# Loads of queries, keys and values moved from SyncE's queue to GpSimd's in an attention and mixing kernel

## The chip, the cores and the metric

The kernel runs on one core of a Trainium2 chip. A core has five engines that work side by side, each through its own instructions in order: TensorE (PE: matrix products, with a weight load ahead of each), VectorE (DVE), ScalarE (ACT), GpSimd (POOL) and SyncE (SP), which here only begins transfers. Transfers run on 16 DMA engines; an instruction on some engine begins one, and a semaphore tells when it has landed. The metric is the device time of one execution in microseconds (us).

## The reference

The program has three stages: attention with pooled queries, a low-rank mixing with a multilayer perceptron, and a gated block with spatial mixing. All is float32 from outside.

```python
# q, k, v: (4, 8, 1152, 64); S = 1152, factor = 2
q_pool = q.reshape(B, H, S // 2, 2, D).mean(axis=3)
scores = (1 / sqrt(D)) * q_pool @ k^T
attn = softmax(scores)                      # sum + 1e-9 in the denominator
x = attn @ v                                # -> (4, 576, 512)
# second stage
h = x^T @ U @ V                             # rank 32 over the sequence
u = x + h^T
x = u + relu(u @ w_ch1) @ w_ch2             # 512 -> 2048 -> 512
# third stage
h = relu(x @ w_in); u, v = halves of h
v_n = (v - mean) / sqrt(var + 1e-6)
out = (u * (w_spatial @ v_n + b_spatial)) @ w_out
```

## The kernel before

The 32 heads are handled as 16 pairs. A pair is nine units of work, one for each 128 rows of pooled queries of one head (the ninth holds the last 64 rows of both heads). The pairs 0 to 4 (`SP = 5`) go another way (`peak`, `turn`, `weigh`); the change concerns the pairs 5 to 15.

For such a pair, `pair_load` begins the transfers of the keys (`kP`, 128 x 1152 float32) and of the queries (`qP`, the two halves to be pooled, 128 x 2 x 576), and `v_load` that of the values (128 x 1152); each is 576 KB. There is one buffer of each kind for these pairs: `r_kraw.items[0]`, the single one of `r_qraw`, and `r_vraw.items[0]`. A load therefore has to wait until the pair before has read its buffer for the last time. `pair_prep` reads keys and queries: ScalarE rounds the keys and VectorE takes the rest (`dve.tensor_sub(kl, raw, kh)`), GpSimd adds the two halves of the queries in place (`pool.tensor_add`), ScalarE and VectorE make a high and a low part of the sum, and GpSimd copies their last columns to `padl`. `v_prep` reads the values: VectorE finds the largest, ScalarE makes the high float16 part and VectorE the low one.

In `scores` TensorE makes the scores of a unit, VectorE finds each row's maximum, ScalarE takes the exponent and rounds it to a high float16 half; the low half is the rest. In units with `lifted(i)` GpSimd makes the low half, in the others VectorE:

```python
act.copy(p16[:, 0, :], p32)
pool.tensor_sub(p16[:, 1, :], p32, p16[:, 0, :])
...
sp.dma_start_transpose(out=pt, in_=p16.rearrange("p a b -> p (a b)"))
```

A transposing transfer, begun by SyncE, turns both halves into `pt`, and `pv` multiplies it by the values on TensorE. Two buffers `p16` and three buffers `pt` go round. Between the units run the perceptron of earlier heads (`mlp1`), its weight loads and its stores to `x2d`, which SyncE begins too.

The order is planned. Nothing is issued at once: `rec` (a `Recorder`) records every operation with its engine, its estimated cost and what it depends on. At the end of the attention stage `issue` plans all recorded operations 83 times (`ORDERS`), each time handing every engine the operation of least key among those that are ready, keeps the best plan, and then walks the list `done` in the planned order and calls the real engine. The instructions of an engine follow each other in that order, and each waits for its semaphores in its turn. In the plan a plain load occupies SyncE for 390 ns and a transposing one for 2790 ns.

All recorded operations are issued from one line, L379, so the profile's groups are told apart by tile: `at` holds the attention's buffers (`kraw`, `qraw`, `vraw`, `p32`, `p16`, `pt` and others), `ml` the perceptron's, `co` small things and weights, `ps` is PSUM, `in_kP_dram`, `in_qP_dram` and `in_v_dram` are the inputs.

Of the kernel before, what the change touches and what calls it, by code (L numbers as in the profile page):

```python
# [24 lines left out]
NP = H // 2  # L25
# [9 lines left out]
SP = 5  # L35
# [56 lines left out]


class Op:
    __slots__ = ("eng", "calls", "cost", "prio", "deps", "users", "left", "ready", "start", "end", "n", "dma", "late", "port", "fly", "lanes", "wide")


class Recorder:
# [51 lines left out]
    def begin(self, eng):  # L150
        op = Op()
        op.eng, op.calls, op.cost, op.prio = eng, [], 0.0, self.prio
        op.deps, op.users, op.n, op.dma, op.start = set(), [], len(self.ops), 0.0, None
        op.port, op.fly, op.lanes, op.wide = False, 0.0, None, False
        self.ops.append(op)
        return op

# [196 lines left out]
    def issue(self, passes=0, later=None):  # L354
        ops, self.ops = self.ops, []
        self.mine = set(ops)
        for op in ops:
            for d in op.deps:
                if d in self.mine:
                    d.users.append(op)  # L360
        key = lambda o: (o.prio, o.n)
        best = None
        for i in range(passes or ITER):
            done, state = self.forward(ops, key)
            end = max(o.end for o in ops)
            if best is None or end < best[0] or i == passes - 1:
                best = (end, done, state, [(o.start, o.end) for o in done])
            self.backward(ops)
            key = (lambda o: (o.late, o.n)) if i % 2 else (lambda o: (o.prio >= 0, o.late, o.n))
        end, done, (self.free, self.dma, self.load, self.port, self.sides), times = best  # L370
        for op, t in zip(done, times):
            op.start, op.end = t
        self.predicted = end
        if later:
            done = self.fill(done, later)
        for op in done:
            eng = getattr(self.nc, op.eng)
            for method, args, kwargs in op.calls:
                getattr(eng, method)(*args, **kwargs)  # L379

# [38 lines left out]
def tile_kernel(ctx: ExitStack, tc: tile.TileContext, qD, kD, qP, kP, v, U, V, w1, w2, w_in, spT, bsp, w_out, out):  # L419
    nc = tc.nc  # L420
    ctx.enter_context(tc.manual_schedule())
    rec = Recorder(nc)
    dve, act, pool, pe, sp = rec.vector, rec.scalar, rec.gpsimd, rec.tensor, rec.sync
# [78 lines left out]
    def flat(t):  # L502
        return t.rearrange("p a b c -> p (a b c)")[:, :2 * KC * D]
# [16 lines left out]
    wide = psum.rearrange("p a b -> p (a b)")  # L520
# [161 lines left out]
    def pair_load(pr):  # L682

        kraw[2 * pr] = t = r_kraw.items[0]
        sp.dma_start(out=t, in_=kP[pr - SP])
        qraw[2 * pr] = t = r_qraw.next()
        sp.dma_start(out=t, in_=qP[pr - SP])

    def pair_prep(pr):

# [33 lines left out]
    def v_load(pr):  # L724
        if pr < SP:
            vraw[pr] = t = r_vraw.items[1] if pr == NP else r_vraw.next()
            src = v[pr // NP, pr % NP].rearrange("p e (c d) -> p e c d", c=KC)
            for e in range(2):
                sp.dma_start(out=t[:, e, :, 0:D], in_=src[:, e])
        else:  # L730
            vraw[pr] = t = flat(r_vraw.items[0]).rearrange("p (e n) -> p e n", e=2)
            sp.dma_start(out=t, in_=v[pr // NP, pr % NP])

    def v_prep(pr):
        if pr < SP:
# [356 lines left out]
    k_load(1)  # L1092
    q_load(1)
    v_load(0)
    rec.prio = 1
    q_prep(1)
# [18 lines left out]
    for pr in range(1, SP):  # L1115
        s0 = 9 * pr
        on(s0 - 9, s0 - 9, k_load, 2 * pr)
        on(s0 - 8, s0 - 8, q_load, 2 * pr)
        on(s0 + 1 if pr == NP else s0 - 7, s0 - 7, v_load, pr)

        on(s0 - 3, s0 - 4, q_prep, 2 * pr)
        on(s0 - 3, s0 - 4, k_prep, 2 * pr)
        on(s0 - 5, s0 - 5, k_load, 2 * pr + 1)
        on(s0 - 3, s0 - 5, q_load, 2 * pr + 1)
        on(s0 + 1, s0, q_prep, 2 * pr + 1)
        on(s0 + 1, s0, k_prep, 2 * pr + 1)
    for pr in range(SP, B * NP):
        s0 = 9 * pr
        t = pr == SP
        on(s0 - 7 if t else s0 - PL, s0 - PL, pair_load, pr)  # L1130
        on(s0 - 7, s0 - 7, v_load, pr)
        on(s0 - 3 if t else s0 - PP, s0 - PP + PQ, pair_prep, pr)
        on(s0 + 1 if t else s0 - VP, s0 - VP + VQ, v_prep, pr)
# [451 lines left out]
```

## Time and profile before

| | us |
|---|---|
| median of 3 runs | 1019.08 |
| lowest and highest of them | 1018.6, 1021.37 |
| the profiled execution | 1017.92 |
| its span in the profile | 1016.2 |
| TensorE busy | 974.9 (96%) |
| VectorE busy | 800.3 (79%) |
| ScalarE busy | 663.9 (65%) |
| GpSimd busy | 256.8 (25%) |

Busy times are sums over the instructions of an engine. Instructions that begin a transfer, semaphore and branch instructions are not counted as busy; they appear with their own times in a timeline (SPq is SyncE's queue). Matmuls are pipelined and their ends are modelled, so a busy TensorE is not one at its peak. Nearly all transfers of this kernel run on one queue, q1, which SyncE feeds: 137.47 MB in 270656 packets, 58.4% of the time of 16 DMA engines.

### The profile page before, as it was taken

To read this page: it belongs to the slowest core of one execution; us is meant where nothing else is said; L and a number is where in the kernel's file an instruction comes from. 1 tells how busy PE (TensorE), PEld (TensorE's weight loads), DVE (VectorE), ACT (ScalarE), POOL (GpSimd) and SP (SyncE) were. 2 spreads that over 40 slices of the span, in tenths; PEclk is the share of its full clock that TensorE was granted. 3 is DMA by queue.
4 is the path that set the end of the run, shared out by engine and by line. 5 is a ranking of instruction groups with operands and counts; after the bars stand their busy time and mean duration, and the time that the engine had idled before them with its cause. 6 is when DMAs were issued, how large, how long until landed. Compare 5 with 4: busy or idle time off the path is not lost.

```text
span 1016.2 us, 26412 instructions
## 1 busy us (share of the span) xinstructions
PE 974.9 (96%) x10983; PEld 803.5 (79%) x10983; DVE 800.3 (79%) x1664; ACT 663.9 (65%) x1238; POOL 256.8 (25%) x213
## 2 busy tenths in 40 slices
PE   7898999999999999999999999999999999999998
PEld 6687788878777877788877787888778788888887
DVE  6978888889998797898677968867598849885670
ACT  7777977787775666766666666656386637575522
POOL 1333532243323413142233323221000003200300
PEclk8999999999999999999999999999999999999999
DMA  9654154299769958788896968677643031531002
GB/s 330 199 182 131 53 172 135 87 217 228 131 123 186 189 111 190 153 156 166 158 192 113 188 118 150 119 146 126 195 137 93 25 135 43 151 99 43 11 2 94
DMA packets 270776, 139.16 MB, mean 137 GB/s; under 512 B 248160, under 2 KB 253152, under 8 KB 269632
## 3 DMA queue, kind: packets, MB, share of 16 engines
q1 hardware_dynamic: 270656, 137.47, 58.4%
q8 instruction: 86, 1.41, 0.6%
q14 instruction: 34, 0.28, 0.1%
HBM read 69.09 MB, written 9.44 MB: 77 GB/s over the span
## 4 chain that ended last, share of the span: by engine, by line
PE 59%; DVE 13%; ACT 8%; DMA 6%; issue 3%; SPq 0%; POOL 0%; ACTq 0%; DVEq 0%
PE ps L379 59%; DVE co L379 6%; ACT at L379 6%; DMA at<-at 5%; DVE at L379 3%; DVE ml L379 3%; ACT ma L379 1%; ACT ml L379 1%; DVE ma L379 1%; DMA ma<-in_bsp_dram 1%; SPq L379 0%; POOL at L379 0%; DMA at<-in_w_dram 0%; ACT co L379 0%; ACT L379 0%
## 5 line engine op out<-in xcount | busy, mean ns | idle before, releaser
L379 PE MATMUL ps<-at,at 128*64 128x65 f32 (+6 forms) x2892 | 240.0, 277 | 9.9 <-ACT at L379 8.3
L379 DVE TENSOR_REDUCE co<-ps 128x1 f32<-128x1152 f32 (+1 forms) x169 | 201.2, 1195 | 52.3 <-PE ps L379 31.5
L379 POOL TENSOR_TENSOR at<-at 128x1152 f16<-128x1152 f32 (+1 forms) x74 | 162.7, 2202 | 285.2 <-ACT at L379 179.4
L379 PEld LDWEIGHTS ps<-at,at 128*64 128x64 f32 (+2 forms) x2892 | 190.6, 160 | 42.6 <-ACT at L379 19.5
L379 PEld LDWEIGHTS <-co 128*128 128x128 f16 x1872 | 177.6, 98 | 53.8 <-issue 15.1
L379 PE MATMUL ps<-ml,co 128*128 128x288 f16 x1344 | 180.3, 286 | 6.2 <-DVE ml L379 4.5
L379 PE MATMUL ps<-ml,ml 128*128 128x288 f16 x1344 | 180.0, 287 | 1.8 <-DVE co L379 1.2
L379 PEld LDWEIGHTS <-ml 128*128 128x128 f16 x1536 | 145.7, 98 | 41.7 <-issue 6.6
L379 ACT ACTIVATE at<-ps,co 128x1152 f32<-128x1152 f32 x99 | 120.7, 1219 | 86.7 <-DVE co L379 80.4
L379 ACT CAST at<-at 128x1152 f16<-128x1152 f32 (+3 forms) x96 | 99.6, 1050 | 20.8 <-DMA at<-at 13.8
L379 PE MATMUL ps<-ma,ma 128*128 128x288 f16 (+2 forms) x676 | 105.0, 318 | 0.0
L379 PEld LDWEIGHTS <-at 128*128 128x128 f16 (+1 forms) x2970 | 89.3, 101 | 10.2 <-issue 5.1
L379 PE MATMUL ps<-at 128*128 128x64 f16 (+1 forms) x2970 | 93.4, 194 | 1.6 <-DVE at L379 0.8
L379 ACT ACTIVATE at<-ps 128x640 f32<-128x640 f32 (+4 forms) x132 | 70.0, 555 | 26.5 <-PE ps L379 25.7
L379 PE MATMUL ps<-at,co 128*128 128x288 f16 (+4 forms) x481 | 72.8, 299 | 0.2 <-DVE at L379 0.2
L379 ACT ACTIVATE at<-at 128x1152 f16<-128x1152 f32 (+1 forms) x55 | 58.6, 1065 | 9.4 <-DMA at<-at 7.7
L379 DVE SCALAR_TENSOR_TENSOR at<-at 128x1152 f16<-128x1152 f32 x44 | 59.4, 1351 | 3.8 <-ACT at L379 2.1
L379 ACT ACTIVATE ml<-ps 128x288 f16<-128x288 f32 (+1 forms) x96 | 38.9, 408 | 31.2 <-PE ps L379 30.8
L379 DVE SCALAR_TENSOR_TENSOR ml<-ml,co,ml 128x288 f16<-128x288 f32 (+1 forms) x80 | 52.9, 686 | 3.0 <-ACT ml L379 3.0
L379 PEld LDWEIGHTS <-ma 128*128 128x128 f16 x448 | 43.7, 98 | 11.4 <-issue 0.5
L379 ACT ACTIVATE ml<-ml,co 128x288 f16<-128x288 f32 (+2 forms) x91 | 47.5, 571 | 6.0 <-DVE co L379 5.7
L379 ACT CAST ma<-ma 128x288 fp32r<-128x288 f32 (+4 forms) x62 | 27.4, 465 | 34.1 <-DVE ma L379 34.1
(108 smaller groups left out, 1278.2 us busy)
## 6 DMA issues: line engine op xcount, KB each, us to landing
ml<-in_w_dram SPq DMA_DIRECT2D x8, 1024.0 KB, 6.3
at<-in_v_dram SPq DMA_DIRECT2D x11, 576.0 KB, 4.7
at<-in_qP_dram SPq DMA_DIRECT2D x11, 576.0 KB, 4.7
at<-in_kP_dram SPq DMA_DIRECT2D x11, 576.0 KB, 5.0
at<-in_qD_dram SPq DMA_DIRECT2D x10, 576.0 KB, 4.4
at<-in_kD_dram SPq DMA_DIRECT2D x10, 576.0 KB, 6.0
ml<-in_w_dram SPq DMA_DIRECT2D x8, 512.0 KB, 5.8
at<-in_w_dram SPq DMA_DIRECT2D x8, 512.0 KB, 4.7
```

Source lines behind the costliest of these rows:

```text
L379: getattr(eng, method)(*args, **kwargs)
```

## The change

`Op` gets one more field, `to`. Where it is set, `issue` calls that engine and not the one that the operation was planned for. `pair_load` sets it to GpSimd for keys and queries, and `v_load` for the values of the pairs from 5 on: 33 loads in all. The plan is made as before, with these loads on SyncE, and the order of the list `done` stays; only the queue is another one. In GpSimd's stream such a load stands between those of GpSimd's operations that the list has before and after it. The source of a load is put into a variable first, which changes nothing that is executed.

```diff
--- before.py
+++ after.py
@@ -92,7 +92,7 @@
 
 
 class Op:
-    __slots__ = ("eng", "calls", "cost", "prio", "deps", "users", "left", "ready", "start", "end", "n", "dma", "late", "port", "fly", "lanes", "wide")
+    __slots__ = ("eng", "calls", "cost", "prio", "deps", "users", "left", "ready", "start", "end", "n", "dma", "late", "port", "fly", "lanes", "wide", "to")
 
 
 class Recorder:
@@ -151,7 +151,7 @@
         op = Op()
         op.eng, op.calls, op.cost, op.prio = eng, [], 0.0, self.prio
         op.deps, op.users, op.n, op.dma, op.start = set(), [], len(self.ops), 0.0, None
-        op.port, op.fly, op.lanes, op.wide = False, 0.0, None, False
+        op.port, op.fly, op.lanes, op.wide, op.to = False, 0.0, None, False, None
         self.ops.append(op)
         return op
 
@@ -374,7 +374,7 @@
         if later:
             done = self.fill(done, later)
         for op in done:
-            eng = getattr(self.nc, op.eng)
+            eng = getattr(self.nc, op.to or op.eng)
             for method, args, kwargs in op.calls:
                 getattr(eng, method)(*args, **kwargs)
 
@@ -682,9 +682,13 @@
     def pair_load(pr):
 
         kraw[2 * pr] = t = r_kraw.items[0]
-        sp.dma_start(out=t, in_=kP[pr - SP])
+        s = kP[pr - SP]
+        sp.dma_start(out=t, in_=s)
+        rec.ops[-1].to = "gpsimd"
         qraw[2 * pr] = t = r_qraw.next()
-        sp.dma_start(out=t, in_=qP[pr - SP])
+        s = qP[pr - SP]
+        sp.dma_start(out=t, in_=s)
+        rec.ops[-1].to = "gpsimd"
 
     def pair_prep(pr):
 
@@ -729,7 +733,9 @@
                 sp.dma_start(out=t[:, e, :, 0:D], in_=src[:, e])
         else:
             vraw[pr] = t = flat(r_vraw.items[0]).rearrange("p (e n) -> p e n", e=2)
-            sp.dma_start(out=t, in_=v[pr // NP, pr % NP])
+            s = v[pr // NP, pr % NP]
+            sp.dma_start(out=t, in_=s)
+            rec.ops[-1].to = "gpsimd"
 
     def v_prep(pr):
         if pr < SP:
```

## Rows read from the trace of the kernel before

**Rows 1.** Window 150 to 720: PE, PEld, DVE, ACT, POOL; clock; DMA

```profile
150.00:720.00 570.00, 553.07 (x7051) 451.17 (x7051) 469.08 (x883) 384.65 (x661) 178.91 (x139) 1.00 0.77 155
```

**Rows 2.** Waits, 150 to 720 us: us in total, times, longest

```profile
POOL at L379 <- DMA at<-in_qP_dram: 26.2, 7, 6.3
ACT at L379 <- DMA at<-at: 21.5, 23, 3.4
PE ps L379 <- DVE co L379: 5.5, 6, 1.4
PE ps L379 <- DVE ml L379: 4.8, 7, 1.4
DVE co L379 <- DMA at<-in_v_dram: 4.0, 3, 2.6
PE ps L379 <- DMA at<-at: 0.7, 2, 0.5
```

**Rows 3.** DMA issues: times, KB each, median us from issue to landing

```profile
at<-in_v_dram SPq DMA_DIRECT2D x11, 576.0 KB, 4.7
at<-at SPq DMA_TRANSPOSE x99, 4.8
```

**Rows 4.** SyncE's instructions on queries: ns min/median/max, first and last start

```profile
L379 SPq DMA_DIRECT2D at<-in_qP_dram x11: 328/382/1476, 162.1 to 565.5; - x11
```

**Rows 5.** SyncE's timeline: start, us, what, times

```profile
473.48 0.53 SPq L379 DMA_DIRECT2D at<-in_v_dram  x1
474.10 0.38 SPq L379 DMA_DIRECT2D at<-in_qP_dram  x1
474.59 5.34 SPq L379 DMA_TRANSPOSE at<-at  x1
479.98 0.57 SPq L379 DMA_DIRECT2D at<-in_kP_dram  x1
480.65 13.26 SPq L379 DMA_TRANSPOSE at<-at  x3
...
519.53 0.53 SPq L379 DMA_DIRECT2D at<-in_v_dram  x1
520.17 4.11 SPq L379 DMA_TRANSPOSE at<-at  x1
...
618.36 51.62 SPq L379 DMA_TRANSPOSE at<-at  x11
```

**Rows 6.** VectorE's timeline: the last readers of load buffers

```profile
249.60 1.35 DVE L379 TENSOR_TENSOR at<-at,at 128x1152 fp32r<-128x1152 f32 x1
...
437.54 1.34 DVE L379 TENSOR_TENSOR at<-at,at 128x1152 fp32r<-128x1152 f32 x1
...
469.11 1.39 DVE L379 SCALAR_TENSOR_TENSOR at<-at,co,at 128x576 f16<-128x576 f32 x1
...
564.72 0.74 DVE L379 SCALAR_TENSOR_TENSOR at<-at,at 128x576 fp32r<-128x576 f32 x1
```

**Rows 7.** GpSimd's timeline, and ScalarE's first reader of queries

```profile
251.21 2.38 POOL L379 TENSOR_TENSOR at<-at 128x1152 f16<-128x1152 f32 x1 [2.97 <-ACT at L379]
...
434.66 1.41 POOL L379 TENSOR_TENSOR at<-at 128x576 f32<-128x576 f32 x1
438.11 3.01 POOL L379 TENSOR_TENSOR at<-at 128x1152 f16<-128x1152 f32 x1 [2.04 <-ACT co L379]
...
565.22 2.48 POOL L379 TENSOR_TENSOR at<-at 128x1152 f16<-128x1152 f32 x1 [7.72 <-ACT at L379]
...
468.30 0.68 ACT L379 ACTIVATE at<-at 128x576 fp32r<-128x576 f32 x1
```

**Rows 8.** Groups by form, 150 to 720: us, mean ns, idle before

```profile
L379 POOL TENSOR_TENSOR at<-at 128x1152 f16<-128x1152 f32 x55 | 133.5, 2430 | 239.4 <-ACT at L379 179.4 <-ACT co L379 37.7 <-DVE co L379 18.1
L379 DVE SCALAR_TENSOR_TENSOR at<-at 128x1152 f16<-128x1152 f32 x44 | 59.4, 1351 | 3.8 <-ACT at L379 2.1 <-ACT co L379 0.9 <-issue 0.4
L379 DVE TENSOR_SCALAR ml<-ml 128x512 int32<-128x512 int32 x12 | 5.8, 487 | 1.2 <-ACT ml L379 1.2
```

## The prediction

> **What bounds the kernel now.** I read the page first, then the window of the stretch that the change touches, then who waits for whom there, and last the single instructions around the loads. The 33 loads that move (queries, keys and values of pairs 5 to 15) and all transposing transfers lie between 150 and 720 us. In these 570 us TensorE is busy 553.07, so 16.9 us of its time are free [rows 1]. That is nearly the whole prize: whatever an edit speeds up here, it can hardly give back more. The list of waits says what TensorE waits for: mostly results of VectorE (5.5 and 4.8 us in the two largest groups) and, for 0.7 us, a transposing transfer [rows 2]. No load stands in it.
>
> The loads are waited for by others: GpSimd stood 26.2 us for queries, VectorE 4.0 us for values [rows 2]. GpSimd's wait looks large, but it has work for 178.91 of the 570 us only [rows 1], and what it waits for isn't urgent: the queries that it adds up at 434.66 are first read by ScalarE at 468.30 [rows 7], 32 us after the addition ended. So the path runs through scores, maximum, exponent, cast, subtraction, transpose and product, and the loads lie beside it.
>
> **Part 1: what SyncE loses.** One issue of a load takes SyncE 0.38 us in the median [rows 4]; 33 of them are 12.5 us of its time. SyncE's queue is worked in order, so a transpose behind a load pays for it only if its data were ready. In most places they weren't. I found three with no other reason: the transpose at 474.59 follows two loads that hold SyncE from 473.48 to 474.48, the one at 480.65 a load that ends at 480.55, the one at 520.17 a load that ends at 520.06 [rows 5]. Without the loads these three start 1.1, 0.7 and 0.6 us sooner, 2.4 us together. What that is worth: ScalarE waited for a transpose 23 times [rows 2], against 99 transposes [rows 3], so about 23 / 99 = 0.23 of such a shift reaches anyone: 0.6 us. Bounds: 0 and 2.4.
>
> **Part 2: loads that begin sooner.** A load waits for the last reader of its buffer. One buffer of values was free at 469.11 + 1.39 = 470.50 [rows 6], and SyncE, busy with transposes, began the load at 473.48 [rows 5]: 3 us late. From GpSimd's queue it can begin when the buffer is free, if GpSimd is. Of VectorE's 4.0 us of waiting for values all may go. VectorE is idle 570 - 469.08 = 100.9 us in the window [rows 1], and TensorE waited 5.5 + 4.8 = 10.3 us for it [rows 2]: 10.3 / 100.9 = 0.10 of an idle microsecond of VectorE is felt. So 0.4 us are gained. Bounds: 0 and 4.0. Queries have 32 us to spare and gain nothing.
>
> **Part 3: what GpSimd gains in work.** No row shows a load begun by GpSimd. Below, the nearest row is SyncE's issue of the same load, 0.38 us [rows 4]; above, GpSimd's own commonest instruction, a subtraction over 128 x 1152, at 2.43 us [rows 8]. I take 1.0 us, near their geometric mean: a begin moves no data through the engine, as the first does, but GpSimd has to make it, as it does the second. That is 33 us in all. What hides it is GpSimd's idleness, 239.4 us ahead of the 55 subtractions alone, 4.4 us each, most of it ended by ScalarE [rows 8]. A load that GpSimd reaches in such a gap is over before ScalarE is done. If the gap is gone, the price is the begin itself plus the wait for the buffer, for all that stands behind it: the subtraction that makes the low half, its transpose, the product on TensorE.
>
> The order is the planned one, so a load stands in GpSimd's stream about where its buffer comes free. I compared such releases with GpSimd's next instruction and found three subtractions close enough to be held: a release at 249.60 + 1.35 = 250.95 against a start at 251.21, one at 437.54 + 1.34 = 438.88 against 438.11, one at 564.72 + 0.74 = 565.46 against 565.22 [rows 6, 7]. With 1.0 us for the begin, the three would start at 251.95, 439.88 and 566.46: 0.7 + 1.8 + 1.2 = 3.7 us of delay, and 0.23 of it, 0.9 us, felt. With 2.43 us it is 2.2 + 3.2 + 2.7 = 8.1. Elsewhere the engine stands idle for longer than a begin after the release.
>
> A load's landing may come later by what the begin takes longer than SyncE's, 0.6 us on the 4.7 us from issue to landing [rows 3]. Its cover for the queries are the 32 us above, for the values the 3 us by which they begin sooner; no wait for keys is among the listed ones. I cost it at nothing; without that cover it is 0.6 us at each place.
>
> **A rule against the change.** VectorE's only wide instructions with one source and both ends in SBUF are twelve of 128 x 512 integers, 5.8 us together [rows 8], 1% of the 570. The Trainium skill (SBUF — State Buffer, the section "SBUF: two separate sides") warns that a transfer begun by GpSimd needs its descriptors written by that engine, and that VectorE in a two-port mode locks it out until its instruction ends. By that rule the sum would grow by 33 x 1% x 0.5 us = 0.2 us, which I leave out; the trace has no such transfer to test it on. A wider reading of it is a rival below.
>
> **Part 4: the transfers themselves.** Bytes and transfers stay. Transposes are the DMA's main load: 11 in a row, with no load among them, take 51.62 us, 4.7 each [rows 5], and the DMA is busy 0.77 of the window [rows 1]. On one queue a load delays the transposes behind it, on two it shares with those in flight; either way the transposes lose the time the load takes once. I cost this at nothing; its cover is that both ways move the same bytes. The Trainium skill (DMA: Bandwidth & Descriptors, "Issuing engines are not separate DMA queues") says the same and adds that issuing from several engines saves only the issuing engine's time. By it Part 2 would shrink to nothing and the sum would be 0.4 us higher.
>
> **The sum.** The profiled execution took 1017.92 us (span 1016.2). 1017.92 - 0.6 - 0.4 + 0.9 = 1017.8. The median of the runs shown, 1019.08, lies 1.2 above the profiled one, so I forecast **1019.0**.
>
> **The rivals.**
> - *GpSimd is held and TensorE feels it* (slower). Place: the three subtractions above. Price: 3.7 to 8.1 us, all of it felt, against nothing gained: 1019.1 + 3.7 = 1022.8 to 1019.1 + 8.1 = 1027.2. It decides from the point where a begin on GpSimd takes over some 2 us, since then the gaps stop hiding others too. For it: the chain is in order on every engine, and GpSimd has ready work behind at 438.11. Against it: TensorE waited 0.7 us for transposes in all [rows 2]. Chance 0.19.
> - *VectorE locks GpSimd out more often* (slower). If any VectorE instruction over two SBUF operands blocks a begin, such as the 44 of 1.35 us [rows 8], each load may take up to 1.35 us longer, 2.35 in all. The three places then cost 2.1 + 3.1 + 2.6 = 7.8 us: 1026.9 if all is felt, 1020.9 at 0.23. Against it: these 44 fill 59.4 of 570 us, a tenth, so most loads miss them. Chance 0.06. The page of the Trainium skill named above states a lock, though not for such instructions against a begin.
> - *SyncE's relief is felt in full* (faster). 2.4 + 4.0 = 6.4 us, nothing lost on GpSimd: 1012.7; with half of it, 1015.9. For it: transposes sit on the path in several places, and ScalarE waited 21.5 us for them [rows 2]. Against it: only three transposes had a load as their last obstacle. Chance 0.17.
> - *Nothing is felt at all*: the loads move, the path doesn't see it, 1019.1. This is the change not doing what it could, and its time lies within the likeliest case.
>
> **How the numbers follow.** The likeliest case (0.58) has its own range of 1016 to 1021.5, from the bounds of Parts 1 to 3 at the shares used. A measurement tells 0.3%, about 3 us, from no change: below 1016.0 counts as faster, above 1022.1 as slower. The likeliest gives 0.53 same, 0.03 faster, 0.02 slower; the held GpSimd 0.03 same and 0.16 slower; the lock-out 0.02 and 0.04; the relief 0.04 same and 0.13 faster. Together: faster 0.16, same 0.62, slower 0.22. The range leaves out the far ends of the two strong rivals: 1014.0 to 1025.0.
>
> **What would show it.** Right: in the profile after, SyncE has no load of these queries, keys and values among its transposes; GpSimd's begins take about 1.0 us each and lie in its gaps; VectorE's wait for values is gone; TensorE's busy time from 150 to 720 stays near 553 of 570. Wrong: begins of over 2 us, subtractions after a begin that start later than ScalarE's cast allows, a new wait of GpSimd for VectorE (the release of a buffer) with ScalarE's wait for transposes growing past 21.5 us, or 11 transposes in a row that take longer than 4.7 us each while a load runs. A gain of over 3 us would mean that SyncE's order held more transposes than the three I found.

## The result and the profile after

The changed kernel takes 1033.76 us (median of 4 runs, 1028.75 to 1034.21), the kernel before 1019.50 on the same chip (4 runs, 1018.60 to 1021.37): a ratio of 1.0123, with a 95% interval of 1.0093 to 1.0153. It is slower by some 14 us, where 1019.0 was forecast and the range ended at 1025.0. The profiled execution took 1033.94 us, with a span of 1032.1.

First the window that answers to [rows 1] (PE, PEld, DVE, ACT, POOL busy; clock; DMA share; GB/s). It is 15 us longer, so that it holds the same work, 7053 matmuls against 7051:

```profile
150.00:735.00 585.00, 560.54 (x7053) 455.81 (x7052) 472.69 (x884) 386.87 (x663) 199.58 (x173) 0.99 0.75 151
```

The 15 us fall into halves. TensorE is idle 585 - 560.54 = 24.5 us, 7.5 more than before, and busy 560.54 - 553.07 = 7.5 us longer for the same products. Most of the second half can be the clock. Of the twelve windows of 50 us between 150 and 750 the granted clock is below 1.00 in four after and in one before (0.97 from 250 to 300). In the trace's record of the clock, the lower of the two levels (1.2 GHz; the upper is 2.4) was granted for 17.1 us in all between 150 and 735 after, and for 3.4 between 150 and 720 before. At half speed 13.7 us more of it cost at most 6.8 us, an estimate from these two figures. Two of the four windows:

```profile
200.00:250.00 50.00, 46.91 (x589) 37.01 (x588) 43.42 (x83) 37.38 (x66) 17.65 (x19) 0.97 0.81 183
...
500.00:550.00 50.00, 45.41 (x540) 36.59 (x538) 33.28 (x61) 27.56 (x47) 15.79 (x15) 0.93 0.84 146
```

The list of waits of the same stretch (us in total, times, longest) answers to [rows 2]:

```profile
ACT at L379 <- DMA at<-at: 28.8, 25, 4.9
POOL at L379 <- DVE at L379: 27.6, 9, 13.1
POOL at L379 <- DMA at<-in_qP_dram: 15.1, 6, 5.1
DVE co L379 <- DMA at<-in_v_dram: 6.9, 3, 3.2
PE ps L379 <- ACT co L379: 6.6, 5, 3.4
PE ps L379 <- DMA at<-at: 1.7, 2, 1.3
```

ScalarE waits 7.3 us longer for transposes, VectorE 2.9 longer for values, and TensorE now waits 6.6 us for ScalarE (1.0 before). The first two are waits for transfers; that the third stands behind such a wait is seen below at its longest place. The issues of the page (median us to landing) and its queues tell the rest, for [rows 3]:

```profile
q1 hardware_dynamic: 265904, 118.01, 51.1%
q0 software_dynamic: 4752, 19.47, 6.3%
...
at<-in_v_dram POOLq DMA_DIRECT2D x11, 576.0 KB, 6.5
...
at<-in_kP_dram POOLq DMA_DIRECT2D x11, 576.0 KB, 5.6
```

The 33 loads are now the 4752 packets of a queue of their own, q0. Values land in 6.5 us where they took 4.7. The begins on GpSimd themselves are short (ns min/median/max, first and last start), in answer to [rows 4]:

```profile
L379 POOL DMA_DIRECT2D at<-in_kP_dram x11: 527/567/577, 167.6 to 593.3; - x11
L379 POOL DMA_DIRECT2D at<-in_qP_dram x11: 527/567/570, 164.1 to 582.4; - x11
```

**One place in full.** TensorE's instructions of the two traces were set beside each other one by one (PE's sequence is the same in both, but for a few neighbours that change places). The changed kernel's lag grows by steps, told here by the time in the kernel before: it is 1.3 us at 116 us, before any moved load, which is scatter, and 1.7 from 136 on; it grows by 1.8 from 172 to 176; by 4.1 from 228 to 256, where the values of pairs 6 and 7 land late; by 0.7 at 339, 1.3 from 386 to 396 and 1.4 from 478 to 480; and, the largest step, by 6.6 us at 525 to 528 of before, 539 to 545 after, of which 0.8 is made up right behind. The steps up to 176 us lie ahead of the first transpose, which begins at 208, so no transpose explains them. In the second a plain load of 1024 KB on SyncE's queue lands 6.92 us after its begin, where it took 6.08, with the keys of pair 5 now beside it on the other queue; ScalarE waits 1.2 us for it, 0.4 before. That was not tested apart. Here is the largest step before, for three loads and the transposes around them (transfers of 514 to 532 us: queue, packets, MB, share of 16 engines; then issues and median landing):

```profile
q1 hardware_dynamic: 7861, 3.75, 98.0%
...
at<-in_qP_dram SPq DMA_DIRECT2D x1, 576.0 KB, 4.5
at<-in_v_dram SPq DMA_DIRECT2D x1, 576.0 KB, 4.8
at<-in_kP_dram SPq DMA_DIRECT2D x1, 576.0 KB, 5.0
...
at<-at SPq DMA_TRANSPOSE x4, 5.4
```

And the same view of the changed kernel, 526 to 546 us:

```profile
q1 hardware_dynamic: 7008, 1.77, 52.5%
q0 software_dynamic: 432, 1.77, 46.5%
...
at<-in_qP_dram POOLq DMA_DIRECT2D x1, 576.0 KB, 4.8
at<-in_v_dram POOLq DMA_DIRECT2D x1, 576.0 KB, 9.5
at<-in_kP_dram POOLq DMA_DIRECT2D x1, 576.0 KB, 8.5
at<-at SPq DMA_TRANSPOSE x3, 11.4
```

The engines are as busy as before (98.0% against 52.5 + 46.5%), but move 3.54 MB in 20 us instead of 3.75 in 18. The 432 packets of the three loads take 0.465 x 16 x 20 = 149 us of engine time, 344 ns each in the mean; over the whole run a packet of q0 takes 0.063 x 16 x 1032.1 / 4752 = 219 ns. Whoever reads the DMA's share alone sees no difference: part of the time goes into packets that take several times the usual 178 ns.

My count of the packets by microsecond shows it (large: a row of a load, 4.5 KB; small: 256 bytes of a transpose, with a few of 4 bytes; mean ns of one):

```
after            loads (q0)      transposes (q1)
531.0 to 532.0   none            1134 at 18
532.0 to 533.0   27 at 876       425 at 19
533.0 to 534.0   19 at 466       43 at 18
534.0 to 535.0   12 at 1248      139 at 36
535.0 to 536.0   15 at 181       41 at 152
536.0 to 537.0   55 at 185       103 at 77
537.0 to 538.0   none            994 at 18
before, one queue
520.0 to 521.0   12 at 1082      587 at 18
521.0 to 522.0   15 at 400       none
522.0 to 523.0   74 at 190       none
523.0 to 524.0   27 at 178       498 at 27
524.0 to 525.0   none            1077 at 18
525.0 to 526.0   16 at 755       767 at 18
526.0 to 527.0   15 at 1050      10 at 40
```

On one queue a load's first rows are slow too (12 at 1082 ns, and 16 at 755 of the next load), but its rows go through in some 4 us, and the transpose behind it follows at full pace. On two, both crawl from 532 to 537, and the last packets of the transpose come in with the last of the load. Slow packets alone don't tell the kernels apart. Over the whole run 941 packets of 4.5 KB took over 300 ns before and 862 after, 547 and 559 us in all, and the time of all packets on q1, or on q0 and q1, is 9498 us before and 9485 after. So the transfers need no more engine time in sum. They land later because two are worked on side by side where one went ahead of the other; that reading is argued from these sums and the one place. The chain that ended last in 524 to 546 us (start, us, what) says what this does:

```profile
526.40 11.41 DMA at<-at
...
537.84 1.46 ACT at L379 x2
...
539.40 6.73 PE ps L379 x49
```

The transpose of 526.40 met the loads of 526.32 and 528.04 and landed after 11.41 us; before, its counterpart at 515.47 took 5.77. ScalarE waits for it, TensorE for ScalarE. The timeline (start, us, what, idle before) shows the three waits that end together, and the clock's part:

```profile
537.61 1.35 DVE L379 TENSOR_REDUCE co<-at 128x1 f32<-128x1152 f32 x1 [3.19 <-DMA at<-in_v_dram]
537.84 1.16 ACT L379 ACTIVATE at<-at 128x1152 f16<-128x1152 f32 x1 [4.21 <-DMA at<-at]
...
539.40 1.33 PE L379 MATMUL ps<-at,at 64*128 64x256 f32 x6 [3.35 <-ACT co L379]
...
542.10 3.78 PE L379 MATMUL ps<-ml,ml 128*128 128x288 f16 x15
```

Those 15 products took 2.00 us before, at 526.21; the granted clock after is 0.58 from 537.80 to 546.00 (before 1.00 throughout), which is mostly the lower level of 1.2 GHz of the two. TensorE stood still for 3.35 us up to 539.40. So one late transpose is paid for twice: in the wait (the lag grows by 3.7 us at 539.40) and in what follows at half clock (2.7 more by 545).

### The profile page after: what moved, and what is told of

The parts are those of the page before. It is cut to its first block, busy times and chain, and to the rows that moved or that the text cites. A ratio compares the mean times of both kernels' runs of the same rounds, so it can differ in the third digit from the quotient of the medians.

```text
span 1032.1 us, 26397 instructions
## 1 busy us (share of the span) xinstructions
PE 982.2 (95%) x10983; PEld 807.7 (78%) x10983; DVE 806.4 (78%) x1664; ACT 665.0 (64%) x1238; POOL 277.2 (27%) x246
## 3 DMA queue, kind: packets, MB, share of 16 engines
q0 software_dynamic: 4752, 19.47, 6.3%
## 4 chain that ended last, share of the span: by engine, by line
PE 53%; DVE 12%; DMA 5%; ACT 4%; issue 2%; POOL 1%; DVEq 0%; ACTq 0%; POOLq 0%; SPq 0%
PE ps L379 53%; DVE co L379 5%; DMA at<-at 5%; DVE at L379 3%; ACT at L379 3%; DVE ml L379 2%; POOL at L379 1%; DMA at<-in_v_dram 1%; DVE ma L379 0%; ACT ml L379 0%; ACT ma L379 0%; DVEq L379 0%; ACT co L379 0%; POOL co L379 0%; ACTq L379 0%
## 5 line engine op out<-in xcount | busy, mean ns | idle before, releaser
L379 PE MATMUL ps<-at,at 128*64 128x65 f32 (+6 forms) x2892 | 242.5, 278 | 16.0 <-ACT at L379 9.0
L379 PEld LDWEIGHTS <-ma 128*128 128x128 f16 x448 | 43.7, 98 | 11.4 <-issue 0.5
```

## The experiments

Two theories. **A**: a load on another queue than the transposes' and a transpose that are in flight together slow each other; the landing comes late, ScalarE and VectorE wait, then TensorE, whose clock falls. **B**: GpSimd is held; a load waits in its stream for the last reader of its buffer, and the subtractions behind it come late. Each ratio is to the kernel before, run on the same chip.

**One kind of load alone.** The line with "gpsimd" is kept for the values only (e1), the queries only (e2), the keys only (e3):

```diff
         sp.dma_start(out=t, in_=s)
-        rec.ops[-1].to = "gpsimd"
```

> Only the values are begun by GpSimd; keys and queries stay with SyncE. Shared transfers (theory A: a load on a queue of its own shares the DMA engines with transposes in flight, both land later, and VectorE, ScalarE and then TensorE wait): values are the loads that VectorE waits for, and their landing grew from 4.6 to 6.6 us in the mean, so most of the loss is here: 1025 to 1031 us. Held GpSimd (theory B: a load waiting for its buffer at the head of GpSimd's stream keeps back the subtractions behind it): values held GpSimd 9.6 us of idle time, a sixth of all, mostly where nothing was ready: 1019 to 1022.

> Only the queries are begun by GpSimd. A: queries have 32 us to spare, so only the transposes that they slow count: 1020 to 1024. B: 19.2 us of idle time ahead of the queries' begins, with casts and subtractions right behind them in several places: 1022 to 1027.

> Only the keys are begun by GpSimd. A: nobody waits for keys, only the transposes that they slow count: 1020 to 1024. B: 26.9 us of idle time ahead of the keys' begins, most of any kind, ended by VectorE: 1023 to 1028.

Measured: values 1025.36 us, ratio 1.0069 (1.0044 to 1.0093); queries 1026.75, 1.0073 (1.0044 to 1.0102); keys 1023.57, 1.0045 (1.0024 to 1.0066). Each kind costs by itself and none carries the loss. The values came out as A expected and not as B did; the queries as B expected, 2.8 us above A's range; the keys in both ranges. The three add up to 1.9%, more than the 1.2% of all together, so the parts aren't independent, and these runs alone don't decide between the theories.

**GpSimd held, the loads on SyncE.** In the place of each load GpSimd clears 550 elements a row of the same buffer, after the same waits, and SyncE begins the load:

```diff
-            eng = getattr(self.nc, op.to or op.eng)
+            eng = getattr(self.nc, op.eng)
+            if op.to is not None:
+                a = op.to if len(op.to.shape) == 2 else op.to[:, 0]
+                self.nc.gpsimd.memset(a[:, :HOLD], 0.0)
```

(`HOLD` is 550, and each load's `to` is now its buffer. By the added lines the fill is L381 and all other operations are L383.)

> GpSimd is held as in the changed kernel, but the transfers go through SyncE's queue as before: at the place of each load in the planned order GpSimd clears 550 elements a row of the buffer (about 0.5 us, with the same wait for the buffer's last reader), and SyncE begins the load behind it. A: 1018 to 1022, since no transfer has a queue of its own. B: 1030 to 1035, as the changed kernel.

Measured: 1021.92, 1.0028 (1.0009 to 1.0047). The 33 fills take 18.5 us, 560 ns each (group by form: us and mean ns; idle before), as long as a begin, and GpSimd waits for VectorE ahead of them as it does in the changed kernel:

```profile
L381 POOL MEMSET at<- 128x550 f32 x33 | 18.5, 560 | 40.6 <-DVE at L383 26.8 <-DVE co L383 8.8 <-ACT ml L383 2.1
```

That lies in A's range, far below B's. Theory B is real, and worth 2.9 us of the 14 (0.9 to 4.8), with what a load loses that begins behind its fill included.

**Another hardware queue.** The 33 loads are begun by ScalarE:

```diff
-        rec.ops[-1].to = "gpsimd"
+        rec.ops[-1].to = "scalar"
```

> The 33 loads are begun by ScalarE in place of GpSimd, at the same places in the planned order: a second queue that GpSimd's software has no part in. A (transfers on another queue than the transposes slow them and are slowed): landings of transposes as in the changed kernel (mean 5.4 us, about a dozen over 6.5), values near 6.6 us, 1026 to 1036 us. If only the queue that GpSimd serves does it: 5.1 us, half a dozen, and 1019 to 1023. B (held GpSimd): GpSimd isn't held; ScalarE is instead, at 65% busy, so 1021 to 1030, with landings as before.

Measured: 1026.17, 1.0070 (1.0045 to 1.0094), about half of the loss with nothing on GpSimd, and in the range of either theory. The transposes whose landing the trace tells (88) took 5.36 us in the mean, 14 of them over 6.5, as A expected, but none over 8.2. The values took 5.6 us in the mean (7 known), not near 6.6. ScalarE's own begins, 33 of some 334 ns, are part of the loss, so this kernel alone doesn't separate queue from engine; the extra loads below do it better.

**Loads a step later in GpSimd's stream.** A load goes behind GpSimd's next instruction unless something needs it first, so that fewer subtractions stand behind a waiting load.

```diff
+            if any(p in op.deps for p in put):
+                while put:
+                    call(put.pop(0))
+            if op.to:
+                put.append(op)
+                continue
+            call(op)
+            if op.eng == "gpsimd":
+                while put:
+                    call(put.pop(0))
```

> As the changed kernel, but each load steps behind GpSimd's next instruction, unless that one needs the load; so a load whose buffer isn't free no longer keeps the subtraction behind it back. A: nothing gained, the queues still meet: 1028 to 1037. B: most of the loss is gone: 1018 to 1024.

Measured: 1069.68, 1.0483 (1.0424 to 1.0542): worse than either theory said. GpSimd's next instruction itself waits, and the load begins that much later. Its waits from 150 to 735 us:

```profile
POOL at L381 <- DMA at<-in_qP_dram: 48.6, 10, 7.8
ACT at L381 <- DMA at<-at: 36.0, 24, 4.4
DVE co L381 <- DMA at<-in_v_dram: 32.0, 9, 6.8
```

VectorE waits 32.0 us for values and GpSimd 48.6 for queries, in the changed kernel 6.9 and 15.1. So a load in a worse place of its stream costs more than all else here. On A against B it says nothing.

**Extra loads in a quiet stretch.** To the kernel before, 14 loads of 576 KB are added, one behind each of the transposes 84 to 97, begun by SyncE, by GpSimd or by ScalarE. They move extra data into the buffers of keys and queries that nobody needs any more (`extra` holds the two buffers and an input for each).

```diff
+                if method == "dma_start_transpose":
+                    turned = getattr(self, "turned", 0)
+                    self.turned = turned + 1
+                    if 83 <= turned < 97:
+                        a, b = self.extra[turned % 2]
+                        self.nc.sync.dma_start(out=a, in_=b)
```

(`gpsimd` and `scalar` in the place of `sync` in the other two.)

> The kernel before with 14 transfers more, of 576 KB each, read by nobody: one behind each of the transposes 84 to 97, in the last units, where the kernel has no loads of its own; begun by SyncE, on the queue of the transposes. A: a load waits for the transpose ahead of it and the next transpose for the load; transposes land in 5 to 6 us, none over 8. Time 1018 to 1023.

> The same 14 transfers at the same places, begun by GpSimd. A: each meets a transpose in flight; these land in 7 us or more, several over 8, and the extra loads in 7 us or more; 1020 to 1030 us. B: transposes land as with SyncE; only GpSimd's subtractions may start later.

> The kernel before with the same 14 extra loads of 576 KB, one behind each of the transposes 84 to 97, this time begun by ScalarE (data that nobody reads). With SyncE's queue the transposes there landed in 5.6 to 8.0 us and the execution took 1034.2 us; with GpSimd's in up to 12.5 us and 1039.6 us. Theory A (a load on any queue other than the transposes' slows the transposes in flight): transposes that meet a load land in 8 to 12 us and the time is 1037 to 1041 us, as with GpSimd. Rival (it is only GpSimd's queue, whose packets come by another way, that disturbs them): landings of at most 8 us and 1033 to 1036 us, as with SyncE. ScalarE's own time for 14 begins, some 14 x 0.6 = 8 us, is in both and may add up to 3 us.

Measured (two runs of each): SyncE 1034.16, 1.0145 (1.0073 to 1.0217); GpSimd 1039.60, 1.0198 (1.0132 to 1.0264); ScalarE 1040.62, 1.0195 (1.0168 to 1.0221). The first two are some 11 and 10 us above the ranges expected, the third is within its own. Most of the extra loads whose landing the trace tells took less than the 7 us expected with GpSimd (8 of 12). The intervals overlap, so the times alone don't part them; the landings do. For the transposes (buffers `at`) begun from 640 to 740 us, us min/median/max from issue to landing, in four kernels: before, SyncE, GpSimd, ScalarE, in this order:

```profile
DMA to landing us min/median/max: 4.5/4.6/5.1
```

```profile
DMA to landing us min/median/max: 4.7/5.8/8.0
```

```profile
DMA to landing us min/median/max: 4.5/7.3/12.5
```

```profile
DMA to landing us min/median/max: 4.6/6.2/11.3
```

(With SyncE the line takes in the extra loads too; the transposes alone are at 6.6 in the median and none is over 8.0.) The same bytes, among the same transposes: on one queue all 16 land later than before, in 5.6 to 8.0 us, and none takes longer; with GpSimd's or ScalarE's queue some land as before, but 8 of 16 and 7 of 17 take over 8 us, up to 12.5 and 11.3. The means are nearer to each other than the longest: 6.8, 7.7 and 7.1 us. It isn't GpSimd's kind of queue that does it; a second hardware queue, q10, in the kernel with ScalarE, does the same:

```profile
q10 hardware_dynamic: 2016, 8.26, 3.1%
```

And the loads aren't free on one queue either, some 14.7 us for 14.

**The loads that met a transpose, and the others.** Fifteen of the 33 loads were picked that met transposes most in the trace of the changed kernel. The expectations below say "in flight for 2.5 us or more", but the split is one of degree. Counted from begin to landing, the 15 had transposes in flight beside them for 4.7 us or more. Of the 18 others ten had so for 3.1 to 5.9 us, two for under 2, and six for nothing. One kernel begins the 15 on GpSimd and the 18 others on SyncE, a second one the reverse:

```diff
-            rec.ops[-1].to = "gpsimd"
+            if pr in (6, 7, 9, 10, 11, 12, 13, 15):
+                rec.ops[-1].to = "gpsimd"
```

(values; queries of 9, 10, 11, 13, 14 and keys of 11, 14 likewise; `not in` for the second)

> Of the 33 loads only the 15 that in the changed kernel's trace met a transpose in flight for 2.5 us or more are begun by GpSimd (the values of pairs 6, 7, 9 to 13 and 15, the queries of 9, 10, 11, 13 and 14, the keys of 11 and 14), the other 18 by SyncE. Theory A (the loss is made where a load on another queue meets a transpose): nearly all of the 14 us stays, 1029 to 1034 us. Theory B (each begin on GpSimd costs, by holding GpSimd, the same wherever it stands): 15 of 33 of the loss, about 1026 us.

> The complement: the 18 loads that met no transpose for as long are begun by GpSimd, the 15 others by SyncE. Theory A: next to nothing is lost, 1019 to 1022 us, and no transpose takes over 8 us to land. Theory B: 18 of 33 of the loss, about 1027 us.

Measured: those that met one 1037.53, 1.0160 (1.0108 to 1.0213); the others 1023.36, 1.0035 (1.0004 to 1.0065). Fifteen loads make the whole loss, more than either theory expected, and the other eighteen about a quarter of it (0.35 of 1.23%, above A's range and below B's). GpSimd's idle time speaks against B as well: in the changed kernel it stood 41.3 us ahead of the begins of the 18 and 14.3 us ahead of those of the 15, so the loads that held it longer cost less. With the 15 the place of above is there again, nearly to the digit (transfers of 524 to 544 us):

```profile
at<-in_v_dram POOLq DMA_DIRECT2D x1, 576.0 KB, 9.3
at<-in_kP_dram POOLq DMA_DIRECT2D x1, 576.0 KB, 8.8
at<-at SPq DMA_TRANSPOSE x3, 11.2
```

What the 18 cost is no more than held GpSimd may cost (0.09 to 0.47% by the run above), but at one place it has A's cause: in their trace the load of the keys of pair 13, at 479.35, had transposes in flight beside it for all of its 6.8 us (timeline; start, us, what):

```profile
475.06 21.64 SPq L379 DMA_TRANSPOSE at<-at  x4
479.35 0.57 POOL L379 DMA_DIRECT2D at<-in_kP_dram  x1 [1.89 <-DVE co L379]
...
486.49 1.15 ACT L379 CAST at<-at 128x1152 f16<-128x1152 f32 x1 [4.98 <-DMA at<-at]
```

One of these four took 11.4 us to land, so "no transpose over 8 us" was missed at this one place, and TensorE's lag grows by 2 to 3.5 us there.

**A plan that knows of it.** The loads are recorded on GpSimd with a cost of 570 ns, and the whole order is planned anew; then the same order with SyncE beginning them:

```diff
-        sp.dma_start(out=t, in_=s)
-        rec.ops[-1].to = "gpsimd"
+        pool.dma_start(out=t, in_=s)
```

(for each of the three kinds; the cost stands in the `Recorder`)

> The change, but with the 33 loads planned on GpSimd at the 570 ns that their begin took, instead of planned on SyncE and moved afterwards; the order of everything else may change with it. Theory B (held GpSimd: a load in the wrong place of its stream keeps back subtractions) expects nearly all of the loss to go: 1018 to 1022 us. Theory A (loads and transposes on two queues slow each other, whatever the place in GpSimd's stream) expects most of it to stay: 1026 to 1034 us, landings of transposes over 8 us as before, and values landing in 6 us or more in the median.

> The order of the replanned kernel (loads planned on GpSimd at 570 ns), but with the 33 loads begun by SyncE where that order has them. It took 1041.1 us with GpSimd's queue. Theory A: the queue makes most of its loss; with SyncE's it falls by some 14 us, to 1024 to 1030 us. Rival (the new order itself is the worse one): it stays at 1035 to 1042 us.

Measured: 1041.06, 1.0205 (1.0188 to 1.0222) with GpSimd, and 1032.13, 1.0110 (1.0075 to 1.0145) with SyncE. Both expectations on the first were too low, and the second lies between its two. The new order is itself worse by 1.1%, which the second run shows, and the move to GpSimd costs 1.0205 / 1.0110, some 0.9%, on top of it: in another order too. Held GpSimd and the queue aren't parted here.

No version was faster than the kernel before.

## Why the prediction was wrong

**Part 4 is the step that failed.** It read: "either way the transposes lose the time the load takes once. I cost this at nothing; its cover is that both ways move the same bytes." The bytes are the same, and in sum the time that the packets take on the engines is too (9498 and 9485 us above). That cover held, but it doesn't cover the cost: what counts is when a transfer lands, and side by side on two queues both land late. For 200 to 745 us I listed from issue to landing for each of the 99 transposes and 10 loads of values:

```
                         transposes: mean, longest, over 6.5 us    values: mean
before                               5.13    7.75     6                    4.63
GpSimd held, SyncE loads             5.19    7.54     8                    4.64
the 18 loads on GpSimd               5.22   11.36    11                    4.70
all 33 on GpSimd                     5.42   12.98    12                    6.62
```

A median hides this: both kernels have 4.8 for the 99 transposes. The difference sits in the longest, 12 against 6 over 6.5 us. That most of the loss comes with the loads' going by another queue, the times at which they then begin included, and not with held GpSimd, is shown by the run that holds GpSimd alone (2.9 of 14 us). That it is made chiefly where a load meets a transpose rests on the runs of the 15 and the 18 and on the landings beside the extra loads; the share that is neither that nor held GpSimd was not measured apart. The step leaned on the Trainium skill (DMA: Bandwidth & Descriptors, "Issuing engines are not separate DMA queues"), which says that transfers begun on several engines interleave on the same 16 DMA engines and that only the issuing engine's time is saved. They do interleave here, but the sentence on time doesn't cover this mix: beginning the loads on a second engine changed the transfers too, by up to 5.64 us (11.41 against 5.77 us).

The second reading in Part 4, 51.62 us for 11 transposes as the DMA's pace [rows 5], was false too. From 640 to 740 us before, a begin takes 2.77 us in the median and a landing 4.6, never over 5.1; 4.7 us is the pace at which the units come. The sign named for being wrong, transposes in a row that take longer than 4.7 us each beside a load, is there: 17.49 us for three from 526.40 on (5.8 each).

**Part 1** expected three transposes to begin 1.1, 0.7 and 0.6 us sooner. SyncE has no such load any more (start, us, what, times):

```profile
465.86 38.94 SPq L379 DMA_TRANSPOSE at<-at  x8
...
526.40 17.49 SPq L379 DMA_TRANSPOSE at<-at  x3
```

But measured against the transpose ahead of it, the first begins 0.2 us sooner, the second 1.5 later and the third no sooner: SyncE is held longer by the begin of the transpose ahead of it (4.65 us for that at 526.40, where its counterpart took 3.97), and landings of 8.42, 11.41 and 12.98 us (5.35, 5.77 and 7.75 before) swallowed the rest. The 0.6 us of gain were not there.

**Part 2** expected the wait for values to go. It grew from 4.0 to 6.9 us. The load of 519.53, now at 528.04, begins 2.4 us sooner beside the transpose ahead of it, as forecast, and lands 2.4 us later (9.55 us after its begin). The cover, "the 3 us by which they begin sooner", was eaten by the failed step.

**Part 3** was right in its mechanism and over-careful in its price: 0.57 us for a begin where 1.0 was taken. The three tight places are seen in GpSimd's timeline (start, us, what, idle before):

```profile
257.98 0.53 POOL L379 DMA_DIRECT2D at<-in_kP_dram  x1 [2.15 <-DVE at L379]
258.53 2.38 POOL L379 TENSOR_TENSOR at<-at 128x1152 f16<-128x1152 f32 x1
...
448.33 2.96 POOL L379 TENSOR_TENSOR at<-at 128x1152 f16<-128x1152 f32 x1 [2.10 <-ACT co L379]
451.23 0.57 POOL L379 DMA_DIRECT2D at<-in_kP_dram  x1
...
582.41 0.57 POOL L379 DMA_DIRECT2D at<-in_qP_dram  x1 [8.54 <-DVE co L379]
583.00 2.39 POOL L379 TENSOR_TENSOR at<-at 128x1152 f16<-128x1152 f32 x1
```

VectorE's last readers of these buffers [rows 6] now are (start, us, what):

```profile
256.33 1.35 DVE L379 TENSOR_TENSOR at<-at,at 128x1152 fp32r<-128x1152 f32 x1
...
447.70 1.35 DVE L379 TENSOR_TENSOR at<-at,at 128x1152 fp32r<-128x1152 f32 x1
...
581.09 0.75 DVE L379 SCALAR_TENSOR_TENSOR at<-at,at 128x576 fp32r<-128x576 f32 x1
```

Shifted by the same amount, the three subtractions of [rows 7] would stand at 257.94, 448.27 and 581.59. They start 0.6, 0.1 and 1.4 us later than that; 0.7, 1.8 and 1.2 were forecast. At the second the planned order has the load behind the subtraction, so the load is late instead, by 2.2 us after its release. What the kernel felt of held GpSimd was 2.9 us (0.9 to 4.8) where 0.9 was forecast, a wider matter than three places: GpSimd waits 27.6 us for VectorE's releases. Still it would have left the time in the range.

**Smaller slips.** One of the 33 loads, the values of pair 5 at 129.2 us, lies ahead of the 150 us that the prediction names; no sum changes by it. The likeliest case's range of 1016 to 1021.5 isn't what its bounds give at the shares used, which is some 1018.1 (0.6 and 0.4 gained, nothing lost) to 1021.0 (8.1 at 0.23 lost, nothing gained). And VectorE's reductions out of SBUF (10 of 128 x 1152 and 12 of 128 x 576, 13.4 and 8.9 us) have one source too and were not in its 1%. None of these is near the 14 us.

**The rivals.** Held GpSimd was the nearest, and for another reason than the right one: its price of up to 8.1 us hung on begins of over 2 us, which took 0.57. That VectorE locks GpSimd out isn't seen: no begin of keys or queries takes over 577 ns in the rows above, none of values over 697. SyncE's relief was not felt. None of the rivals had a transfer that slows another one.

## What to carry to other kernels

Before a load is moved to another engine's queue, look in the trace for what is in flight at the moment it would begin: a queue also keeps transfers apart. At the place above a plain load that followed the transpose on its queue left it at 5.77 us, where the same load beside it made it 11.41. The load is not free in either way: 14 extra ones cost some 15 us on the transposes' queue and some 20 on another. Look at the longest landings and the sum of waits for them, not at the median, and not at the DMA's busy share, which was the same here with the transfers landing later. And count a late transfer with what follows it: here up to 6.8 us went at the lower clock, beside 7.5 more of idleness.

## What was not expected of the hardware

A plain load of 576 KB on one queue and a transposing transfer on another slow each other: 9.55 and 11.41 us instead of 4.77 and 5.77, with packets of the load at 466 to 1248 ns in three microseconds in a row, where the median of the run is 178. (On one queue only the first packets of a load were as slow there, 755 to 1082 ns.) It happens with GpSimd's queue and with ScalarE's, to landings of 12.5 and 11.3 us. The sum of the packets' time hardly changes by it. Which part of the transfer engines makes the packets wait stays open; no run here could look into it. A begin on GpSimd is 0.57 us for 128 rows of 4.5 KB, hardly more than SyncE's 0.53 for the same values [rows 5].
